# Products with V raised in the scheduler's order, and a third staging buffer for weights

## The chip, the cores and the metric

One core of a Trainium2 chip runs the whole program. The metric is the device time of one execution in microseconds (us), from the first to the last instruction and what lies around them. TensorE (PE) does the matmuls, VectorE (DVE) and ScalarE (ACT) the elementwise work, GpSimd (POOL) next to nothing here; SyncE (SP) issues nearly all DMAs. Each engine takes its own instructions in the order in which they were laid down when the program was built.

## What is computed

Causal attention over 4 batches of 8 heads, 576 positions, head size 64, mixed with a linear memory, and behind it two feed-forward blocks (FFN) on the 2304 resulting rows of width 512:

```python
scores = scale * q @ k.T            # causal mask, softmax
local = a @ v
q_p = phi(q)                        # elu(q) + 1
mem_out = (q_p @ M_prev) / (q_p @ z_prev + 1e-06)
x = g * mem_out + (1 - g) * local   # g = sigmoid(beta) per head
x = softplus(x @ w_in) @ w_out      # 512 -> 2048 -> 512
x = relu(x @ w_in2) ** 2 @ w_out2   # 512 -> 2048 -> 512
```

q, k, v, M_prev, z_prev are 32-bit floats. The weights come as 64-bit words; each is turned into a 32-bit float and split into a high and a low 16-bit half. Other operands of matmuls are split likewise, and a product is three matmuls (high by high, high by low, low by high), summed in PSUM.

## The kernel before

**Attention.** The rows are cut into 18 chunks of 128 (8 for each pair of batches, and a ninth that holds the last 64 rows of both). `CH`, `EXT` and `GRP` list them: a chunk has `EXT` = 128 to 640 key positions in reach, and its 8 heads are done in steps of `GRP` heads (4, 2 or 1, so that a step has about 512 columns). `prep_k`, `prep_q`, `prep_phi`, `prep_v` and `prep_m` cast, split and transpose a chunk's inputs, one part of the next chunk at a time between the steps. The loads go into tiles of one buffer each in the pool `att`, issued from SP; for chunk 1, k, q and v go into extra tiles in the pool `stage`, so that they need not wait for those of chunk 0.

**A step.** `emit_s` (line 281) computes a head's scores on PE into one of two banks of `s_ps` (306), lets DVE add the mask and take the row minimum (311), and ACT take the exponential with its row sum (315); the result is in `Pt`, two buffers. `emit_p` (320) splits it (ACT 327, DVE 328) and transposes it into `PT`, four buffers: for chunks 0 and 1 with PE and an ACT copy (196, 197), for all others with a transposing DMA from SP (190). `emit_pv` (335) stands `LAG` = 4 steps behind in the program. At a chunk's first head it calls `prep_n` (258), the memory norm: 16 matmuls `nps` (264) into a PSUM tile of the pool `mm`, whose three buffers the PE transposes use too, and three DVE steps (270 to 272) into `cc`. Then it does the memory products (343) and the products with V (351) into `pvt`, a tile of one buffer for four heads. After four heads `emit_x` (362) scales `pvt` on DVE into `xt` (371), which frees `pvt`, adds the two parts (378), and after eight heads splits the sum (382, 383) and transposes it to x.

**Feed-forward.** The first FFN runs in blocks of 256 rows (two chunks). A unit `h` is 24 matmuls on W1 (431 to 433) and the softplus on ACT and DVE (435 to 442); a block has eight. A unit `x` is 96 matmuls on W2 (448 to 450); for block 0 the same work stands in four quarters `xq` (485 to 487), 48 matmuls each, so that quarter a needs only the weight pieces 8a to 8a + 7 and those before. The 32 weight pieces of 512 KB are loaded by `load_piece` into `wst` (`NST` = 2 buffers, pool `stage`) and split by `split_piece` (404) with DVE (414, 415, 416, 419) and ACT (418) by way of `wcv`, two buffers. The load of piece i + `NST` is written right behind the split of piece i. The second FFN (702 to 722) starts when the first has ended.

**The order of the work.** A loop at the end of the function writes the steps of attention and the FFN units of earlier blocks in turn, in shares by estimated time. The build then runs a list scheduler with a model of times: at each moment an engine takes, of what the model holds to be ready, the instruction that stands first. `tc.high_priority(n)` lets what is written inside stand as if it were n instructions earlier in the program. Weight splits have 2000 (`HW`), `emit_x` 200 (`HXE`), scores 50 (`HS`), the split and transpose of p 50 (`HP`). Products with V, with all of `emit_pv`, and the FFN units have none. The result is one fixed order for each engine.

Of the kernel before, what the change touches and what calls it, by code (L numbers as in the profile page):

```python
# [21 lines left out]
FR = 0.4  # L22
W1R = 1
B1Q = 3
HS, HP, HXE, HW = 50, 50, 200, 2000

LOE = 99
TQ = 2
# [4 lines left out]
KVB = 9  # L33
SPB = 2
WCB = 2
NST = 2
PTB = 4
PB = 2
P16 = 2
# [4 lines left out]
def kernel(  # L44
# [49 lines left out]

    stage_cm = tc.tile_pool(name="stage", bufs=NST, reuse_waits="tile")
    w1_cm = tc.tile_pool(name="w1", bufs=1, side="right", reuse_waits="tile")
# [16 lines left out]
    stage = stage_cm.__enter__()  # L113
# [45 lines left out]
    def segs(g):  # L159
        x = CH[g]  # L160
        if len(x) == 2:
            return [(x[0], P * x[1], 0, P)]
        return [(2 * x[0] + i, 4 * P, i * R, R) for i in range(2)]

    def lo_eng(g):
        return dve if g < LOE else pool

    def load(nm, g, pool_=None):
        if g >= NC or (nm, g) in raw:
            return  # L170
        src = {"q": q, "k": k, "v": v}[nm]
        t = (pool_ or att).tile([P, H, D], F32, name="raw" + nm, bufs=1)
        for b, s0, r0, n in segs(g):
            sp.dma_start(out=t[r0:r0 + n], in_=src[b, :, s0:s0 + n, :].rearrange("h p d -> p h d"))
        raw[nm, g] = t
    def load_m(g):
        for b, s0, r0, n in (segs(g) if g < NC else []):
            if s0 == 0:
                t = att.tile([P, EMAX], F32, tag="Pt", name="mraw", bufs=PB)[:, :HD].rearrange("p (h d) -> p h d", h=H)
                for i in range(2):  # L180
                    sp.dma_start(out=t[i * D:(i + 1) * D], in_=M_prev[b].rearrange("h d e -> d h e"))
                raw["m", g] = t

    def transp(g, out, in_, lim):
        nblk = in_.shape[1] // P
        if g >= lim:
            step = nblk if nblk <= 12 else nblk // 2
            for a in range(0, nblk, step):
                e = a + step
                sp.dma_start_transpose(out=out[:, a:e], in_=in_[:, a * P:e * P])  # L190
            return
        for a in range(0, nblk, 8):
            e = min(nblk, a + 8)
            ps = mm.tile([P, 8, P], F16, tag="mm", name="tps")
            for i in range(a, e):
                pe.transpose(ps[:, i - a], in_[:, i * P:(i + 1) * P], ident)
            act.activation(out[:, a:e], ps[:, :e - a], AF.Copy)

    def prep_q(g):
        r = raw["q", g]  # L200
        qT[g] = att.tile([P, 2 * H, P], F16, name="qT", bufs=2)
        if g < TP:
            qn = att.tile([P, H, 2, D], F16, tag="qn", name="qn")
            act.activation(qn[:, :, 0, :], r, AF.Copy)
            lo_eng(g).tensor_tensor(qn[:, :, 1, :], r, qn[:, :, 0, :], ALU.subtract)
            transp(g, qT[g][:, :H], qn.rearrange("p h t d -> p (h t d)"), TP)
            ps = mm.tile([P, H, P], F16, tag="mm", name="tps")
            for h in range(H):
                for t in range(2):
                    pe.transpose(ps[t * D:(t + 1) * D, h], qn[:, h, 1 - t], ident)  # L210
            act.activation(qT[g][:, H:], ps, AF.Copy)
            return
        qn = att.tile([P, 2, H, 2, D], F16, name="qn")
        act.activation(qn[:, 0, :, 0, :], r, AF.Copy)
        lo_eng(g).tensor_tensor(qn[:, 0, :, 1, :], r, qn[:, 0, :, 0, :], ALU.subtract)
        dve.tensor_copy(qn[:, 1, :, 1, :], qn[:, 0, :, 0, :])
        dve.tensor_copy(qn[:, 1, :, 0, :], qn[:, 0, :, 1, :])
        transp(g, qT[g], qn.rearrange("p a h t d -> p (a h t d)"), TP)
# [9 lines left out]
    def prep_v(g):  # L228
        r = raw.pop(("v", g))
        V[g] = att.tile([P, 2, H, D], F16, name="V", bufs=KVB)  # L230
        act.activation(V[g][:, 0], r, AF.Copy)
        dve.tensor_tensor(V[g][:, 1], r, V[g][:, 0], ALU.subtract)
# [12 lines left out]
    def prep_phi(g):  # L245
        r = raw.pop(("q", g))
        e = att.tile([P, H, D], F32, tag="prod", name="phie")
        act.activation(e, r, AF.Relu, scale=-1.0)
        act.activation(e, e, AF.Exp, scale=-1.0)
        f = att.tile([P, H, D], F32, name="phi")  # L250
        dve.scalar_tensor_tensor(f, r, 0.0, e, ALU.max, ALU.add)
        fn = att.tile([P, H, 2, D], F16, name="phin")
        act.activation(fn[:, :, 0, :], f, AF.Copy)
        lo_eng(g).tensor_tensor(fn[:, :, 1, :], f, fn[:, :, 0, :], ALU.subtract)
        phiT[g] = att.tile([P, H, P], F16, name="phiT", bufs=2)
        transp(g, phiT[g], fn.rearrange("p h t d -> p (h t d)"), TP)

    def prep_n(g):
        ps = mm.tile([P, H], F32, tag="mm", name="nps")
        for b, s0, r0, n in segs(g):  # L260
            for h in range(H):
                for t in range(2):
                    i = b * H + h
                    pe.matmul(
                        ps[r0:r0 + n, h:h + 1], phiT[g][:, h, r0:r0 + n], zc[:, t, i:i + 1],
                        start=(t == 0), stop=(t == 1),
                    )
        cc = att.tile([P, 2, 2, H // 2], F32, name="cc", bufs=3)
        c2 = cc[:, :, 1, :]
        dve.tensor_scalar(c2, ps.rearrange("p (a h) -> p a h", a=2), 1.0e-6, None, ALU.add)  # L270
        dve.reciprocal(c2, c2)
        dve.tensor_tensor(c2, c2, gM.rearrange("p (a h) -> p a h", a=2), ALU.mult)
        cc_t[g] = cc

    def kblocks(g):
        x = CH[g]
        if len(x) == 2:
            return [[POS[x[0], i]] for i in range(x[1] + 1)]
        return [[POS[2 * x[0] + j, i] for j in range(2)] for i in range(4)] + [[g]]
# [55 lines left out]
    def emit_pv(g, h):  # L335
        if h == 0:
            prep_n(g)
        if h % 4 == 0:
            pvt[g] = pvp.tile([P, 2, H // 2, D], F32, name="pvt")
        for t in range(2):  # L340
            for b, s0, r0, n in segs(g):
                o = pvt[g][r0:r0 + n, 1, h % 4]
                pe.matmul(o, phiT[g][:, h, r0:r0 + n], Mt[b][:, t, h, :], start=(t == 0), stop=(t == 1))
        o = pvt[g][:, 0, h % 4]
        t, o0, nb = PT.pop((g, h))
        for i, ks in enumerate(kblocks(g)):
            n = P // len(ks)
            for y, z in ((0, 0), (0, 1), (nb, 0)):
                for x, kb in enumerate(ks):
                    r = slice(x * n, (x + 1) * n)  # L350
                    pe.matmul(  # L351
                        o[r], t[:, o0 + i + y, r], V[kb][:, z, h, :],
                        start=(i == 0 and y + z == 0), stop=(i == nb - 1 and y > 0),
                    )
# [143 lines left out]
    load("k", 0)  # L498
    load("q", 0)
    load("k", 1, stage)  # L500
    load("q", 1, stage)
    load("v", 0)
    gates()
    z_setup()
# [22 lines left out]
    prep_k(0)  # L527
    prep_q(0)
    prep_phi(0)
    prep_v(0)  # L530
    load_m(0)
    load("v", 1, stage)
    for i in range(NST):
        pieces[i] = load_piece(order[i], (moe_w_in, moe_w_out), sp, stage)
    prep_m(0)
# [8 lines left out]
    def attn_step(s):  # L544
        if s < len(steps):
            g, h = steps[s]
            G = GRP[g]
            with tc.high_priority(HS):
                emit_s(g, h)
            nst = H // G  # L550
            i = h // G
            for part in range(4):
                if part * nst // 4 == i:
                    prep_part(g + 1, part)
            with tc.high_priority(HP):
                emit_p(g, h)
        for g, h0 in pv_at.get(s, ()):
            for h in range(h0, h0 + GRP[g]):
                emit_pv(g, h)
                if h % 4 == 3:  # L560
                    with tc.high_priority(HXE):
                        emit_x(g, h // 4)
# [25 lines left out]
    def run_unit(u):  # L588
# [8 lines left out]
        else:  # L597
            i = u[1]
            with tc.high_priority(HW):
                split_piece(order[i], pieces.pop(i), (W1, W2), stage, on_pool=False)  # L600
            if i + NST < 2 * NPC:
                pieces[i + NST] = load_piece(order[i + NST], (moe_w_in, moe_w_out), sp, stage)

    s = nw = 0
    while s <= ready_step(0):
        attn_step(s)
        s += 1
        while nw < 2 * NPC and nw < W1R * s:
            run_unit(("w", nw))
            nw += 1  # L610
# [82 lines left out]
    while t0 < NT:  # L693
# [3 lines left out]
        for f in range(NFC):  # L697
# [10 lines left out]
            g = [bp.tile([P, 512], F16, name=f"gg{t}_{f}", bufs=1) for t in range(2)]  # L708
# [47 lines left out]
```

## Time and profile before

| | |
|---|---|
| median of 3 runs | 1000.85 us (997.05 to 1002.72) |
| the profiled execution's own time | 1001.6 us |
| its span, first to last instruction | 999.8 us |
| mean granted TensorE clock | 0.953 |
| PE busy | 911.8 us (91%) |
| DVE busy | 583.1 us (58%) |
| ACT busy | 545.2 us (55%) |
| DMA moved | 101.00 MB |

A matmul's busy time overlaps with that of its neighbours, so the time of a line on PE is not to be added to that of another; the busy time of the whole engine is. The clock is a share of full speed: 1.0 is the upper level of 2.4 GHz, 0.5 the lower of 1.2. The page cuts the span into 40 slices of 25 us. In a timeline, a row has the start, the length, the engine and line, the operation, what it writes from what, and in brackets how long the engine was idle before it and what ended that. SPq is SP's queue of DMA issues.

### The profile page before, as it was taken

The numbers are of one execution on the slowest core, as the hardware profiler recorded it, in microseconds if no ns is written. First come the engines' busy times: TensorE is split into PE (matmuls) and PEld (weight loads), VectorE is DVE, ScalarE is ACT, GpSimd is POOL, SyncE is SP. The second block draws the span as 40 slices with busy tenths as digits, with TensorE's granted clock in tenths as the row PEclk, the third lists the DMA queues.
The fourth block names the chain that finished last, engine by engine and source line by source line (L and its number), as shares of the span: only waits on it lengthen the run. The fifth ranks groups of instructions, "written<-read, shape, count | busy, mean of one in ns | idle before, by whom it ended". The sixth has DMA issues, their size and how long they took to land.

```text
span 999.8 us, 20668 instructions
## 1 busy us (share of the span) xinstructions
PE 911.8 (91%) x8436; PEld 642.3 (64%) x8436; DVE 583.1 (58%) x1359; ACT 545.2 (55%) x1090; POOL 2.2 (0%) x10
## 2 busy tenths in 40 slices
PE   3335988899999999999999999999999999999998
PEld 2234877788678888999887887444444444444483
DVE  6888998878546786767756399980240141042040
ACT  8765787779548696867867284640340241142050
POOL 0000000000000000000000000000000000000000
PEclk8555999999899999999999999999999999999999
DMA  9999898787568985655743365520000000000000
GB/s 202 215 221 226 179 165 177 140 125 126 98 99 134 191 156 109 110 83 95 126 86 65 87 205 170 171 82 32 11 1 22 22 1 11 32 1 11 22 13 22
DMA packets 283216, 101.00 MB, mean 101 GB/s; under 512 B 248048, under 2 KB 280816, under 8 KB 283120
## 3 DMA queue, kind: packets, MB, share of 16 engines
q1 hardware_dynamic: 282880, 99.65, 49.3%
q8 instruction: 66, 1.08, 0.5%
q14 instruction: 30, 0.25, 0.1%
q10 hardware_dynamic: 240, 0.02, 0.0%
HBM read 48.78 MB, written 4.72 MB: 54 GB/s over the span
## 4 chain that ended last, share of the span: by engine, by line
PE 65%; DMA 12%; DVE 12%; ACT 7%; issue 3%; SPq 1%; ACTq 0%; DVEq 0%
PE h2ps L703 6%; PE h2ps L704 6%; PE h2ps L702 6%; PE ops L718 6%; PE ops L720 6%; PE ops L719 6%; PE xps L448 4%; PE xps L449 4%; PE xps L450 4%; PE s_ps L306 4%; PE hps L431 3%; PE hps L432 3%; PE hps L433 3%; DMA rawk<-in_k_dram 2%; PE pvt L351 2%
## 5 line engine op out<-in xcount | busy, mean ns | idle before, releaser
L709 DVE CAST gg<-r 128x512 f16<-128x512 f32 (+1 forms) x80 | 32.0, 399 | 232.5 <-ACT r L707 206.7
L431 PE MATMUL hps<-x,W 128*128 128x256 f16 x576 | 157.9, 274 | 2.7 <-DMA x<-xn 1.6
L433 PE MATMUL hps<-x,W 128*128 128x256 f16 x576 | 157.8, 274 | 0.1
L432 PE MATMUL hps<-x,W 128*128 128x256 f16 x576 | 157.9, 274 | 0.0
L448 PE MATMUL xps<-g,W 128*128 128x256 f16 x512 | 139.8, 276 | 3.2 <-ACT g L441 3.1
L449 PE MATMUL xps<-g,W 128*128 128x256 f16 x512 | 140.4, 275 | 1.6 <-DVE g L442 1.6
L450 PE MATMUL xps<-g,W 128*128 128x256 f16 x512 | 140.5, 276 | 0.0
L306 PE MATMUL s_ps<-KT,qT 128*128 128x128 f16 (+2 forms) x992 | 94.6, 227 | 38.9 <-DVE cs L311 34.7
L315 ACT ACTIVATE Pt<-Pt,cs 128x128 f32<-128x128 f32 (+4 forms) x144 | 84.2, 585 | 66.9 <-DVE cs L311 66.6
L704 PE MATMUL h2ps<-x,W 128*128 128x512 f16 (+1 forms) x320 | 114.5, 358 | 0.0
L702 PE MATMUL h2ps<-x,W 128*128 128x512 f16 (+1 forms) x320 | 114.5, 358 | 0.0
L703 PE MATMUL h2ps<-x,W 128*128 128x512 f16 (+1 forms) x320 | 114.5, 358 | 0.0
L719 PE MATMUL ops<-W,gg 128*128 128x512 bf16 x288 | 109.0, 379 | 0.0
L720 PE MATMUL ops<-W,gg 128*128 128x512 f16 x288 | 109.0, 379 | 0.0
L718 PE MATMUL ops<-W,gg 128*128 128x512 f16 x288 | 108.5, 379 | 0.0
L722 ACT ACTIVATE osb<-ops 128x512 f32<-128x512 f32 x18 | 10.7, 597 | 169.3 <-PE ops L720 169.3
L306 PEld LDWEIGHTS <-qT 128*128 128x128 f16 (+1 forms) x992 | 64.5, 106 | 55.4 <-issue 42.0
L328 DVE TENSOR_TENSOR p<-Pt,p 128x512 f16<-128x512 f32 (+2 forms) x104 | 69.1, 665 | 28.0 <-ACT p L327 27.4
L706 ACT ACTIVATE r<-h2ps 128x512 f32<-128x512 f32 (+1 forms) x80 | 44.1, 552 | 75.2 <-PE h2ps L704 75.1
L351 PE MATMUL pvt<-V,PT 128*128 128x64 f16 (+1 forms) x1392 | 65.8, 198 | 12.8 <-DMA PT<-p 10.7
L311 DVE CUSTOM_DVE_ANT_0 Pt<-s_ps,mask 128x128 f32<-128x128 f32 (+3 forms) x128 | 61.9, 483 | 12.3 <-PE s_ps L306 11.6
L327 ACT ACTIVATE p<-Pt 128x512 f16<-128x512 f32 (+2 forms) x104 | 63.1, 607 | 9.4 <-DMA PT<-p 8.0
(117 smaller groups left out, 1642.7 us busy)
## 6 DMA issues: line engine op xcount, KB each, us to landing
wst<-in_moe_w_in_dram SPq DMA_DIRECT2D x32, 512.0 KB, 4.7
wst<-in_moe_w_out_dram SPq DMA_DIRECT2D x32, 512.0 KB, 4.2
rawk<-in_k_dram SPq DMA_DIRECT2D x16, 256.0 KB, 4.1
rawq<-in_q_dram SPq DMA_DIRECT2D x16, 256.0 KB, 4.1
rawv<-in_v_dram SPq DMA_DIRECT2D x16, 256.0 KB, 4.3
out_dram<-osb SPq DMA_DIRECT2D x16, 256.0 KB, 2.0
PT<-p SPq DMA_TRANSPOSE x100, 3.4
mraw<-in_M_prev_dram SPq DMA_DIRECT2D x8, 128.0 KB, 4.3
```

The lines of the kernel that those rows point to most:

```text
L306: pe.matmul(o[x * n:(x + 1) * n], qT[g][:, t * H + h, x * n:(x + 1) * n], KT[kb][:, h, a - j * P:e - j * P], start=(t == 0), stop=(t == 1),)
L431: pe.matmul(o, wh, x[:, c], start=(c == 0), stop=False)
L432: pe.matmul(o, wh, x[:, NCC + c], start=False, stop=False)
L433: pe.matmul(o, wl, x[:, c], start=False, stop=(c == NCC - 1))
L448: pe.matmul(ps, wh, gh, start=(f == f0), stop=False)
L449: pe.matmul(ps, wh, gl, start=False, stop=False)
L450: pe.matmul(ps, wl, gh, start=False, stop=(f == f1 - 1))
L702: pe.matmul(ps[:, :n], wh, xh, start=(c == 0), stop=False)
L703: pe.matmul(ps[:, :n], wh, xl, start=False, stop=False)
L704: pe.matmul(ps[:, :n], wl, xh, start=False, stop=(c == NCC - 1))
L719: pe.matmul(ps, gh, W4[1][:, f, :], start=False, stop=False)
L720: pe.matmul(ps, gl, W4[0][:, f, :], start=False, stop=(f == NFC - 1))
```

## The change

Scores stand 100 instructions earlier instead of 50. All that `emit_pv` writes gets a block of its own at 300. `NST` goes from 2 to 3. q and v of chunk 1 are loaded into the usual tiles of `att` instead of extra tiles in `stage`, and their loads are written behind the last reader of chunk 0's: q behind `prep_phi(0)`, v behind `prep_v(0)` as before. k of chunk 1 keeps its extra tile. In space, the two tiles of 2 KB a partition that go from `stage` make room for the third `wst` of 4 KB.

```diff
-HS, HP, HXE, HW = 50, 50, 200, 2000
+HS = 100
+HP = 50
+HXE = 200
+HW = 2000
+HV = 300
...
-NST = 2
+NST = 3
...
     load("k", 1, stage)
-    load("q", 1, stage)
     load("v", 0)
...
     prep_phi(0)
+    load("q", 1)
     prep_v(0)
     load_m(0)
-    load("v", 1, stage)
+    load("v", 1)
...
             for h in range(h0, h0 + GRP[g]):
-                emit_pv(g, h)
+                with tc.high_priority(HV):
+                    emit_pv(g, h)
                 if h % 4 == 3:
                     with tc.high_priority(HXE):
                         emit_x(g, h // 4)
```

## Rows read from the trace of the kernel before

**Rows 1.** The page, 40 slices of the span: granted TensorE clock in tenths.

```profile
PEclk8555999999899999999999999999999999999999
```

**Rows 2.** Windows: length; busy us of PE, PEld, DVE, ACT, POOL; clock; DMA; GB/s.

```profile
0.00:93.80 93.80, 35.21 (x378) 26.86 (x379) 76.48 (x209) 62.86 (x139) 2.23 (x10) 0.58 1.05 213
93.80:262.00 168.20, 154.79 (x1982) 135.74 (x1982) 147.12 (x352) 132.86 (x268) 0.00 (x0) 0.97 0.80 152
262.00:400.00 138.00, 130.61 (x1539) 109.19 (x1538) 87.12 (x236) 89.61 (x203) 0.00 (x0) 1.00 0.80 135
400.00:566.00 166.00, 164.26 (x2246) 145.19 (x2245) 109.75 (x256) 118.50 (x236) 0.00 (x0) 1.00 0.51 89
566.00:999.80 433.80, 426.91 (x2298) 225.35 (x2296) 162.61 (x310) 141.37 (x246) 0.00 (x0) 0.99 0.16 51
```

**Rows 3.** Timeline of PE, 26 to 112 us.

```profile
33.09 0.34 PE L351 MATMUL pvt<-V,PT 128*128 128x64 f16 x3 [1.83 <-ACT PT L197]
...
51.35 0.61 PE L264 MATMUL nps<-zc,phiT 128*128 128x1 f16 x16
...
63.12 0.29 PE L343 MATMUL pvt<-Mt,phiT 128*128 128x64 f16 x2 [1.23 <-DVE xt L371]
...
78.68 0.29 PE L343 MATMUL pvt<-Mt,phiT 128*128 128x64 f16 x2 [2.38 <-DVE xt L371]
...
93.82 0.37 PE L431 MATMUL hps<-x,W 128*128 128x256 f16 x1 [1.11 <-ACT x L197]
...
97.18 0.42 PE L432 MATMUL hps<-x,W 128*128 128x256 f16 x1
...
97.56 0.27 PE L431 MATMUL hps<-x,W 128*128 128x256 f16 x1
...
100.73 0.27 PE L433 MATMUL hps<-x,W 128*128 128x256 f16 x1
```

**Rows 4.** Timeline of DVE, 30 to 130 us.

```profile
55.98 0.16 DVE L272 TENSOR_TENSOR cc<-cc,gM 128x8 f32<-128x8 f32 x1
...
57.41 0.68 DVE L371 TENSOR_TENSOR xt<-pvt,cc 128x512 f32<-128x512 f32 x1
```

**Rows 5.** DMA issues, 400 to 566 us: tile, operation, count, median us to landing.

```profile
PT<-p SPq DMA_TRANSPOSE x39, 3.2
```

**Rows 6.** Timeline of ACT, 53 to 94 us.

```profile
53.79 1.00 ACT L197 ACTIVATE PT<-tps 128x1024 f16<-128x1024 f16 x1
...
92.74 1.02 ACT L197 ACTIVATE x<-tps 128x1024 f16<-128x1024 f16 x1 [0.67 <-PE tps L196]
```

**Rows 7.** Timeline of DVE: last pass of the eighth and of the sixteenth weight piece.

```profile
54.52 0.66 DVE L419 TENSOR_TENSOR W<-wcv,W 128x512 bf16<-128x512 f32 x1
...
96.32 0.68 DVE L419 TENSOR_TENSOR W<-wcv,W 128x512 bf16<-128x512 f32 x1
```

**Rows 8.** PE's waits, 117 to 400 us: total us, times, longest.

```profile
PE pvt L351 <- DMA PT<-p: 10.7, 14, 1.3
```

**Rows 9.** DMA issues, 117 to 400 us.

```profile
PT<-p SPq DMA_TRANSPOSE x54, 3.6
```

**Rows 10.** PE's waits, 0 to 93.8 us.

```profile
PE s_ps L306 <- DVE cs L311: 30.3, 21, 5.7
```

**Rows 11.** DVE's waits, 0 to 93.8 us.

```profile
DVE wcv L414 <- DMA wst<-in_moe_w_out_dram: 4.9, 4, 2.0
```

**Rows 12.** Timeline of all engines, 0 to 70 us.

```profile
3.79 0.97 SPq L174 DMA_DIRECT2D rawq<-in_q_dram  x1
...
8.24 0.69 DVE L251 SCALAR_TENSOR_TENSOR phi<-rawq,phie 128x512 f32<-128x512 f32 x1 [0.49 <-ACT phie L249]
...
25.79 0.37 PE L306 MATMUL s_ps<-KT,qT 128*128 128x128 f16 x2 [1.58 <-ACT V L231]
```

**Rows 13.** DMA issues, 0 to 93.8 us: KB each, median us to landing.

```profile
rawq<-in_q_dram SPq DMA_DIRECT2D x5, 256.0 KB, 5.1
```

## The prediction, made before the change was run

> **What bounds the kernel now.** I read the slices of the page first, then the windows, then the timeline of each engine around the places where the windows change character.
>
> The clock row is the quickest sight of the shape [rows 1]: TensorE was granted half speed in slices 2 to 4, full speed from then on. The windows tell why [rows 2]. Until 93.8 us PE is busy 35.21 us of 93.8, so 58.6 us are idle; from 93.8 to 262 it idles 13.4 us, from 262 to 400 7.4 us, from 400 to 566 1.7 us, and behind that 6.9 us. From 93.8 us on the end is set by the sum of PE's work, and only idle PE time can be taken out. Two thirds of that lies ahead of 93.8 us, where the first matmul of the first FFN block starts [rows 3]. So the question is what that matmul waits for, and how much work is ready when it starts sooner.
>
> It waits for the x of chunks 0 and 1, and that comes late for one reason which the timeline shows. The products with V of chunk 0's first half run at 33.09 us. The 16 tiny matmuls of the memory norm (nps, line 264), written just ahead of them, run at 51.35 us [rows 3]; the DVE line that needs them (272) follows at 55.98, and xt, which empties the only pvt tile, at 57.41 us [rows 4]. All other products of chunks 0 and 1 stand behind that: chunk 1's first at 63.12, its last half at 78.68 [rows 3].
>
> **Products with V at 300.** The block now holds all that `emit_pv` issues: nps and its three DVE steps, the memory products and the products with V. From 400 to 566 us there are 2246 matmuls, 256 DVE and 236 ACT instructions [rows 2] for 39 transposes of p, one a step [rows 5]: 70 a step. 300 is 4.3 steps, and the products stand 4 steps behind their scores: they will run as soon as their transposed p is there.
>
> At the start this is the gain. With nps no longer at 51, xt of chunk 0 moves to the thirties, pvt is free, and chunk 1's last half waits for its own p alone. ACT copies that p's transpose at 53.79 [rows 6], done at 54.8. Today it is 15.1 us from the start of that half's products (78.68) to the end of the last copy of x (92.74 + 1.02) [rows 3, 6]; I keep these 15.1, since DVE is as full as before, and get 70 us. The first FFN matmul starts about 24 us sooner.
>
> What can run then? One quarter of block 0: 2 units of 24 matmuls on W1 and 48 on W2, on the first eight weight pieces, the last of which is ready at 54.52 + 0.68 us [rows 7]. The second quarter wants the sixteenth piece, at 96.32 today. At full clock 29 matmuls go from 97.56 to 100.73 us, 0.109 us each [rows 3]; 96 of them are **10.5 us** of PE work moved into idle time. That is the main term. Its bounds: 0 if the order does not move, 10.5 on today's pieces.
>
> The clock adds a little. From 93.82 to 97.18 us 16 matmuls went at 0.21 each [rows 3], so 1.7 us are lost in the warm-up, which would now fall into idle time: **1.7 us**, between 0 and 4.5 (half of the 8.9 us that PE works in 24 us at the share of the first window).
>
> At the back the same edit costs. Between 117 and 400 us products already stand at the landing: 14 waits for the transposed p, 10.7 us, among 54 transposes [rows 8, 9]. From 400 to 566 us PE's waits hold none of this kind, and now the 39 transposes there come to stand so too. Bounds: 0, and 0.76 us (the mean wait) for each of 39, 29.8 us. Taken: as often as in the earlier stretch (14 of 54), but landing takes 3.2 us there against 3.6 [rows 5, 9]; so 0.36 us for 10 of them, **3.6 us**.
>
> **Scores at 100 in place of 50.** This moves scores, mask step and exp up by 0.7 of a step, past p's split and the preparations on DVE and ACT. PE waits 30.3 us for DVE's mask step in the first stretch [rows 10], with nothing else to do. Two Pt buffers hold the scores to two steps ahead. If the scores win more DVE turns, p and prepared chunks are later. I take 0: it helps the start that is counted above and does not raise the work that is ready. Bounds 2 us either way (three turns of 0.68, the copy's length in [rows 7]).
>
> **Three staging buffers.** Eight pieces take 41.8 us, from 54.52 to 96.32, 5.2 us each [rows 7]. A third in flight could bring the sixteenth and later pieces forward, and with them the other quarters. Bounds: 0, and the 13.4 us that PE idles from 93.8 to 262. Nearest row: in the first window DVE waited 4.9 us in all for pieces of w_out [rows 11]; I take **4 us**. The price is on DVE: splits stand ahead of all else, DVE is busy 76.48 of 93.8 us, and each early piece pushes attention back by its four passes (up to 2.7 us at 0.68). Even three of them leave x at 78 us, and the 10.5 us still fit before 93.8.
>
> **q and v of chunk 1 in the usual buffers.** q's load is issued at 3.79 us today [rows 12]. Now it waits until phi of chunk 0 has read rawq (8.24 + 0.69), and lands 5.1 us later [rows 13], at 14.0. The scores of chunk 1 start at 25.79 [rows 12]: 12 us of cover. If that were gone, the cost is 5 us. v follows its chunk's split likewise, and is wanted at 63.12 now, in the forties then. The later loads of q and v shift by the same few us, under the same cover. On SP these loads and a third weight load come into one queue ahead of transposes; I cost this at nothing here because PE is idle there. The space balances.
>
> **Sum.** 10.5 + 1.7 + 4 - 3.6 = 12.6 us less than the profiled execution's 1001.6 us: 989.0. That execution was 0.75 over the median 1000.85, so **988**.
>
> **Rivals.**
> *The gain is given back, or never made.* The weights set the pace: the DMA engines' share is 1.05 up to 93.8 us and 0.80 up to 262 [rows 2], so a third load only shares them. Then later quarters start when they do now, the 10.5 us that ran early are missing behind, PE idles that much more, and the time is 1000. For it speaks the share; against it, the 4.9 us of DVE's wait [rows 11], little beside 93.8. The Trainium skill (Perfetto Trace Analysis, What "DMA-bound" means) says that where the DMA engines bind, larger descriptors are what matters; by it the third buffer alone brings nothing and the sum would be 992. Here the shares agree that they are full, but the short DVE wait does not. Also here: nps takes its PSUM tile from the pool of the PE transposes, three buffers; if it still gets none before 51 us, the start stays at 93.8 and only 4 and 3.6 remain, 1000. Together 0.18.
>
> *Slower: PE stands at the products.* The engine runs in order, so a product placed at its landing holds up the FFN matmuls behind it. Place: the steps from 400 us on. Price: up to 29.8 us; with 12.2 us still won at the start, 1018. It turns the sign by more than 0.5% from 17.2 us on, 0.44 us for each of the 39. For it: the slack there, which this edit removes, is why no wait is seen. Against: where the products stand at the landing already, three of four do not wait. The Trainium skill (DMA: Bandwidth & Descriptors, Queues, rings and completion order) has each DMA engine take a ring's descriptors in order, so that a transpose waits behind a load issued before it on SP. The trace agrees in direction, 3.6 us with loads about and 3.2 with few. Chance 0.19.
>
> *More than forecast.* The third buffer brings the whole 13.4 us and the clock 4.5: 972. This is part of the faster share.
>
> **How the numbers follow.** Faster by over 0.5% (about what a measurement of this kernel can tell, 5 us: below 995.8) has my forecast and the larger gain, 0.63; within it the first rival, 0.18; slower the second, 0.19. The range goes from the larger gain, less 2 us for the spread of runs, 970, to the upper edge of no change, 1006, plus the same 2: 1008. Alone, the forecast's own range is 972 to 996.
>
> **What would show it.** Right: nps before 40 us, xt before 42, the first FFN matmul between 62 and 80, PE busy over 45 us up to 93.8, the sixteenth piece before 92, the last scores' landing waits from 400 us on below 8 us in all. Wrong: the first FFN matmul still after 88; or that start, but PE idle from 93.8 to 262 over 24 us (first rival); or waits for the transposed p over 28 us in the whole trace (second). If PE's idle time in the first 93.8 us falls and the end does not, I have mistaken where the work was short.

## The result, and the profile after

The changed kernel takes 992.37 us (median of 12 runs, 989.44 to 1001.07), the kernel before 1001.89 in the same comparison: a ratio of 0.9908 (0.9882 to 0.9934), some 9 us faster. The profiled execution of after has an own time of 997.09 us and a span of 995.3, so it lies 4.7 us above its median, and the two profiles side by side show only 4.5 us of the gain.

First the windows of after, with the columns of [rows 2]; the edges are the same but for the end.

```profile
0.00:93.80 93.80, 39.91 (x401) 30.27 (x402) 81.14 (x226) 64.95 (x144) 2.23 (x10) 0.98 1.13 228
93.80:262.00 168.20, 154.78 (x1982) 135.58 (x1981) 143.58 (x334) 129.61 (x263) 0.00 (x0) 0.95 0.80 148
262.00:400.00 138.00, 130.48 (x1661) 115.13 (x1660) 94.35 (x256) 97.02 (x217) 0.00 (x0) 1.00 0.79 135
400.00:566.00 166.00, 161.35 (x2149) 140.23 (x2147) 106.39 (x243) 111.58 (x225) 0.00 (x0) 0.98 0.57 96
566.00:995.30 429.30, 421.12 (x2234) 220.94 (x2250) 159.45 (x303) 140.00 (x245) 0.00 (x0) 0.99 0.15 47
```

PE idles 53.9, 13.4, 7.5, 4.7 and 8.2 us in the five windows, against 58.6, 13.4, 7.4, 1.7 and 6.9 before. The first window gave 4.7 us, not the 12 forecast, and the fourth took 3 back. The clock of the first window, 0.98 against 0.58, is no gain: the first clock record of after stands at 85.8 us, and the page takes the clock as full where it has none. The first FFN matmuls of after still follow one another at 0.21 us (three from 90.79 to 91.43) and last 0.42, as those from 93.82 to 97.18 in [rows 3] did before the full clock came; that is the lower level, 1.2 GHz. (In the last window 18 matmul records are missing, 8418 for 8436; at 0.22 us each they are 4 us of the 8.2.)

The timeline of PE in after, 26 to 92 us; line numbers are 5 higher than before:

```profile
26.24 0.34 PE L356 MATMUL pvt<-V,PT 128*128 128x64 f16 x3 [0.86 <-ACT PT L202]
...
49.36 0.29 PE L201 MATMUL tps<-ident,p 128*128 128x128 f16 x1 [0.62 <-ACT p L332]
49.44 0.61 PE L269 MATMUL nps<-zc,phiT 128*128 128x1 f16 x16
...
57.67 0.27 PE L348 MATMUL pvt<-Mt,phiT 128*128 128x64 f16 x2 [0.62 <-DVE xt L376]
...
77.04 0.29 PE L348 MATMUL pvt<-Mt,phiT 128*128 128x64 f16 x2 [0.62 <-DVE xt L376]
...
90.79 0.42 PE L436 MATMUL hps<-x,W 128*128 128x256 f16 x1
...
91.43 0.42 PE L436 MATMUL hps<-x,W 128*128 128x256 f16 x1
```

Beside [rows 3]: the products of chunk 0's first half moved from 33.09 to 26.24 us. That is not the work of their priority. The same row in two kernels of the experiments below, products_alone (before with the priority) and after_no_products (after without it):

```profile
32.73 0.34 PE L352 MATMUL pvt<-V,PT 128*128 128x64 f16 x3 [0.93 <-ACT PT L198]
```

```profile
26.23 0.34 PE L356 MATMUL pvt<-V,PT 128*128 128x64 f16 x3 [0.86 <-ACT PT L202]
```

The memory norm nps moved from 51.35 to 49.44 only. So chunk 1's products still stand behind it (57.67 for 63.12, the last half 77.04 for 78.68), and the first FFN matmul came from 93.82 to 90.79, 3.0 us earlier, not 24.

The timeline of DVE in after (last pass of the eighth weight piece, xt of chunk 0, last pass of the sixteenth piece), and then one row of before:

```profile
47.07 0.69 DVE L424 TENSOR_TENSOR W<-wcv,W 128x512 bf16<-128x512 f32 x1
...
56.93 0.69 DVE L376 TENSOR_TENSOR xt<-pvt,cc 128x512 f32<-128x512 f32 x1
...
95.20 0.68 DVE L424 TENSOR_TENSOR W<-wcv,W 128x512 bf16<-128x512 f32 x1
```

```profile
105.08 0.69 DVE L419 TENSOR_TENSOR W<-wcv,W 128x512 bf16<-128x512 f32 x1
```

xt stands at 56.93 for 57.41 [rows 4]. The last row corrects the prediction: its sixteenth piece at 96.32 [rows 7] was the fifteenth; counted through, the sixteenth ends at 105.8 before and 95.9 after, 9.9 us sooner. (So the 41.8 us between the two rows of [rows 7] are seven pieces of 6.0 us, and not eight of 5.2.)

The waits in after that answer to [rows 8] (PE, 117 to 400 us), to "none of this kind" (PE, 400 to 566), to [rows 10] and to [rows 11] (PE up to 91, DVE up to 93.8), and the transposes of [rows 9] and [rows 5]:

```profile
PE pvt L356 <- DMA PT<-p: 11.1, 14, 1.8
```

```profile
PE pvt L356 <- DMA PT<-p: 4.5, 8, 0.8
```

```profile
PE s_ps L311 <- DVE cs L316: 32.3, 21, 4.3
```

```profile
DVE wcv L419 <- DMA wst<-in_moe_w_in_dram: 0.2, 1, 0.2
```

```profile
PT<-p SPq DMA_TRANSPOSE x55, 3.3
```

```profile
PT<-p SPq DMA_TRANSPOSE x36, 3.2
```

Products now stand at the landing behind 400 us too: 8 of 36 wait there, 4.5 us. DVE's wait for pieces of w_out, 4.9 us, is gone, and one of 0.2 us remains. PE's wait for the mask step on DVE is as long as before.

### The profile page after: what moved, and what is told of

Same layout as the page of the kernel before. It is cut to its first block, busy times and chain, and to the rows that moved or that the text cites. A ratio compares the mean times of both kernels' runs of the same rounds, so it can differ in the third digit from the quotient of the medians.

```text
span 995.3 us, 20666 instructions
## 1 busy us (share of the span) xinstructions
PE 907.6 (91%) x8418; PEld 642.2 (65%) x8436; DVE 584.9 (59%) x1359; ACT 543.2 (55%) x1090; POOL 2.2 (0%) x10
## 4 chain that ended last, share of the span: by engine, by line
PE 67%; DMA 14%; DVE 9%; ACT 5%; issue 3%; SPq 1%; ACTq 0%; DVEq 0%
PE ops L726 7%; DMA PT<-p 6%; PE h2ps L710 6%; PE h2ps L709 6%; PE h2ps L708 6%; PE ops L724 6%; PE ops L725 6%; PE xps L454 4%; PE xps L455 4%; PE xps L453 4%; PE s_ps L311 3%; PE hps L438 3%; PE hps L437 3%; PE hps L436 3%; PE pvt L356 3%
## 5 line engine op out<-in xcount | busy, mean ns | idle before, releaser
L436 PE MATMUL hps<-x,W 128*128 128x256 f16 x576 | 160.1, 278 | 3.5 <-DVE cc L275 2.1
L438 PE MATMUL hps<-x,W 128*128 128x256 f16 x576 | 160.0, 278 | 0.0
L437 PE MATMUL hps<-x,W 128*128 128x256 f16 x576 | 160.0, 278 | 0.0
L311 PE MATMUL s_ps<-KT,qT 128*128 128x128 f16 (+2 forms) x992 | 83.8, 225 | 35.9 <-DVE cs L316 35.3
L725 PE MATMUL ops<-W,gg 128*128 128x512 bf16 x270 | 102.3, 379 | 0.0
L311 PEld LDWEIGHTS <-qT 128*128 128x128 f16 (+1 forms) x992 | 59.2, 105 | 47.7 <-issue 43.1
L356 PE MATMUL pvt<-V,PT 128*128 128x64 f16 (+1 forms) x1392 | 62.1, 199 | 16.7 <-DMA PT<-p 15.6
```

The lines of the kernel that those rows point to most:

```text
L311: pe.matmul(o[x * n:(x + 1) * n], qT[g][:, t * H + h, x * n:(x + 1) * n], KT[kb][:, h, a - j * P:e - j * P], start=(t == 0), stop=(t == 1),)
L436: pe.matmul(o, wh, x[:, c], start=(c == 0), stop=False)
L437: pe.matmul(o, wh, x[:, NCC + c], start=False, stop=False)
L438: pe.matmul(o, wl, x[:, c], start=False, stop=(c == NCC - 1))
```

## The experiments

**How the tables are read.** The stretch behind the last W2 matmul of the first FFN is 377.6 to 377.8 us in every kernel here whose numbers are given, so the difference lies ahead of it. From the first FFN matmul to that one, I took the time from each matmul's start to the next and subtracted the pace of its kind at full clock (0.1095 us for the FFN's 256 columns, 0.0535 for scores of 128, 0.0285 for products with V or with the memory, 0.026 for nps). What is left over is put under one cause: PE at 1.2 GHz (by the clock records); a gap of over 0.15 us; or a step between a matmul with 64 columns of weights and one with 128 (below). The number of cases is in parentheses; "nps" and "first FFN" are starts in us, "last W2" is the end of that stretch, the three columns between are lost us. Each row is one profiled execution, and such a one lies up to 5 us off its median (after 4.7 above, loads_alone 4.2 below), so differences of a few us in it are no results. Two things stand in no column. In nine of the kernels (all but before, after, buffer_alone and the two with every norm early) the clock records begin only after the first FFN matmul; there the first 15 to 26 matmuls at 0.21 us, 1.5 to 2.6 us, are missing from "half clock". And matmuls with 64 columns that stand together run faster than the pace taken here (see the steps between widths).

| kernel | nps | first FFN | half clock | gaps | 64/128 steps | last W2 |
|---|---|---|---|---|---|---|
| before | 51.4 | 93.8 | 6.0 | 29.7 (33) | 20.2 (193) | 622.1 |
| after | 49.4 | 90.8 | 13.4 | 34.0 (36) | 10.1 (103) | 617.7 |
| products_alone | 47.0 | 92.7 | 4.9 | 32.7 | 11.2 (113) | 614.0 |
| scores_alone | 51.3 | 93.0 | 6.7 | 29.7 | 14.5 (142) | 616.9 |
| buffer_alone | 49.3 | 93.6 | 7.8 | 22.8 | 16.6 (159) | 611.0 |
| loads_alone | 42.9 | 90.9 | 4.9 | 20.1 (21) | 15.2 (149) | 602.4 |
| after_no_products | 49.4 | 93.4 | 9.0 | 26.7 | 14.7 (142) | 616.2 |
| after_two_buffers | 42.8 | 91.4 | 10.5 | 35.4 | 12.1 (119) | 622.3 |
| after_norm01 | 15.1 | 74.7 | 11.4 | 46.2 (44) | 11.1 (111) | 618.1 |
| after_norm_early | 15.1 | 77.6 | 42.6 | 48.4 | 13.8 (138) | 654.4 |
| before_norm_early | 17.1 | 72.0 | 59.4 | 74.7 | 17.2 (166) | 695.6 |
| scores_ext | 50.3 | 91.7 | 4.8 | 29.3 (30) | 7.6 (78) | 603.7 |
| loads_scores_ext | 42.9 | 90.9 | 3.1 | 22.7 (22) | 7.9 (82) | 594.7 |
| scores_51 | 51.3 | 93.1 | 8.6 | 27.8 | 19.6 (186) | 624.0 |

All these kernels compute everything that the reference does. Each ratio is to the kernel before in the same comparison, with its 95% interval.

**One part at a time.** *products_alone*, on before:

```diff
+HV = 300
-                emit_pv(g, h)
+                with tc.high_priority(HV):
+                    emit_pv(g, h)
```

> The kernel before with the block at 300 round emit_pv alone. The whole change gave a ratio of 0.9908, 9.5 us, though nps stayed at 49 us and the first FFN matmul moved only from 93.8 to 90.8. Theory A (the gain is the products': attention ends about 10 us sooner and PE has no long stretch without ready work): ratio 0.990 to 0.994, last product with V near 555 us in place of 565. Theory B (the gain is the third buffer's): ratio 0.998 to 1.004, and the products at their landing cost something at the back. Theory C (scores at 100 make it): same as B here.

Measured: 994.12 us, 0.9938 (0.9914 to 0.9962). Waits for the transposed p from 91 to 620 us: 20.4 us in 22, against 10.7 in 14 before. So the products do come to their landing and lose 10 us there, and the kernel is faster all the same: the ratio is in the range of theory A, and the last product with V starts at 557.5 us for 565.1 before. The start explains 1.1 us of it; the largest change in the table is the steps between widths, 9.0 us less.

*scores_alone*, on before: `HS` 50 becomes 100.

> The kernel before with scores at 100 alone. Theory C: ratio 0.990 to 0.994. Theories A and B: 0.998 to 1.003, with PE's waits for the mask step in the first 93.8 us (30.3 us) as long as before within 3 us.

Measured: 995.97 us, 0.9950 (0.9930 to 0.9969). Costed at nothing, it is worth 5 us alone, between the ranges of the theories; PE's wait for the mask step is 29.5 us, as before. The start moved 0.8 us, gaps not at all, the steps between widths from 20.2 to 14.5.

*buffer_alone* has `NST` 3 and the moved loads of q and v of chunk 1, as shown; *loads_alone* has the moved loads and two buffers, so it lacks the first two lines:

```diff
-NST = 2
+NST = 3
...
-    load("q", 1, stage)
...
     prep_phi(0)
+    load("q", 1)
...
-    load("v", 1, stage)
+    load("v", 1)
```

> The kernel before with three staging buffers and the loads of q and v of chunk 1 moved, no priorities changed. Theory B: ratio 0.990 to 0.994, the 32nd weight piece 8 us or more before 194 us. Theories A and C: 0.996 to 1.002.

> The kernel before with the loads of q and v of chunk 1 moved and two staging buffers. All theories: 0.998 to 1.003, the cover of 12 us over q holds; if the later q is on the path, the first score of chunk 1 comes up to 5 us after 25.8 us and the ratio is 1.003 to 1.006.

Measured: buffer_alone 990.02 us, 0.9898 (0.9871 to 0.9926), at the edge of theory B; loads_alone 986.09, 0.9850 (0.9820 to 0.9880). The part that I costed at nothing is the largest of the change, outside every range that I had given for it, and on top of it the third buffer costs 4 us. Where it starts is seen on SP's queue, first in before (behind the row at 3.79 us of [rows 12]), then in loads_alone:

```profile
4.80 1.18 SPq L174 DMA_DIRECT2D rawv<-in_v_dram  x1
6.02 1.83 SPq L181 DMA_DIRECT2D mraw<-in_M_prev_dram  x2
7.89 0.62 SPq L174 DMA_DIRECT2D rawv<-in_v_dram  x1
8.56 1.81 SPq L395 DMA_DIRECT2D wst<-in_moe_w_in_dram  x2
```

```profile
3.86 0.97 SPq L174 DMA_DIRECT2D rawv<-in_v_dram  x1
4.87 1.85 SPq L181 DMA_DIRECT2D mraw<-in_M_prev_dram  x2
6.76 1.17 SPq L395 DMA_DIRECT2D wst<-in_moe_w_in_dram  x2
```

The rows at 3.79 and 7.89 are chunk 1's q and v for the extra tiles; both are gone from there. V of chunk 0 is issued 0.9 us sooner, the first pieces 1.8. Then the attention's chain of steps carries it on. These are the last mask steps of chunk 0 on DVE, of before, of loads_alone and of buffer_alone:

```profile
25.45 0.28 DVE L311 CUSTOM_DVE_ANT_0 Pt<-s_ps,mask 128x128 f32<-128x128 f32 x1
```

```profile
23.59 0.28 DVE L311 CUSTOM_DVE_ANT_0 Pt<-s_ps,mask 128x128 f32<-128x128 f32 x1
```

```profile
28.46 0.29 DVE L311 CUSTOM_DVE_ANT_0 Pt<-s_ps,mask 128x128 f32<-128x128 f32 x1
```

With the loads alone they end 1.9 us sooner and nps starts 8.5 us sooner; with a third buffer, three pieces come to DVE ahead of the mask steps, which end 4.9 us later than with two, and nps falls back to 49.3. In all kernels but products_alone and the three with an earlier norm, the start of nps goes with the loads and the buffers (42.8 or 42.9, 49.3 or 49.4, and 50.3 to 51.4 where nothing of either is done), and not with the priority of the products. Behind the start, loads_alone loses 9.6 us less in gaps and 5.0 less in steps between widths. Why a start 3 us earlier leaves so many fewer gaps was not tried further, so beyond the start the cause of the 14.5 us is open.

**One part taken out of the change.** *after_no_products* is after without the block at 300, *after_two_buffers* is after with `NST` 2.

> The changed kernel without the block round emit_pv. Theory: the products' priority wins steps between 64 and 128 columns and loses as much in waits for the transposed p (15.6 us in 22 waits behind 91 us against 3.6 in 5 with the buffer alone): ratio to the kernel before 0.988 to 0.993, the same as the changed kernel within 0.3%, waits under 9 us, steps over 130. Rival (the products' priority is worth its 6 us here too): 0.994 to 0.998.

> The changed kernel with two staging buffers. Loads moved alone gave 0.985, loads moved with the third buffer 0.990. Theory: the third buffer costs about 4 us, and without it the change gives 0.983 to 0.988. Rival (the third buffer gives what the prediction credits it with): 0.992 to 0.997.

Measured: after_no_products 997.24 us, 0.9973 (0.9951 to 0.9994); after_two_buffers 998.22, 0.9984 (0.9964 to 1.0005). Within the change, the priority of the products is worth 6.5 us (0.9973 to 0.9908) and the third buffer 7.6 (0.9984 to 0.9908), though the same buffer cost 4 in buffer_alone. Both kernels missed what I expected: after_no_products came out in its rival's range, after_two_buffers above both of its ranges. after_no_products differs from buffer_alone in `HS` alone: there scores at 100 cost 7.5 us (0.9898 to 0.9973), while alone they gave 5. Only the products' priority has the same price in both places, 6.5 us alone and 6.5 within. For the buffer and the scores each edit deals a new order, and the price depends on the rest of it.

**Is it the order of nps that holds the start?** *after_norm01* writes the memory norm of chunks 0 and 1 right behind their `prep_phi` and leaves all else of the change as it is:

```diff
-        if h == 0:
+        if h == 0 and g > 1:
             prep_n(g)
...
             prep_phi(g)
+            if g == 1:
+                prep_n(g)
...
     prep_phi(0)
+    prep_n(0)
```

> The changed kernel with the memory norm of chunks 0 and 1 alone written behind prep_phi; all other chunks as in the changed kernel. Written early for all chunks, nps of chunk 0 ran at 15 us and the first FFN matmul at 78, but the end came 38 us later, with FFN units and transposes held up all along. Theory P (the tail came from nps holding PSUM tiles of mm ahead of the FFN units in the written order, chunk after chunk; the early start itself pays as the prediction had it): first FFN matmul between 62 and 80, ratio to the kernel before 0.976 to 0.986. Rival G (an early start is given back: until the next pieces and chunks are there PE has one quarter to do, then idles and falls to half clock): first FFN matmul between 62 and 80, but PE idles over 12 us between that and 150 us (3.1 in the changed kernel from 91 on), ratio 0.988 or more.

Measured: 997.87 us, 0.9961 (0.9943 to 0.9979), 5 us worse than after. Its timeline of PE:

```profile
12.61 1.06 PE L201 MATMUL tps<-ident,phin 128*128 128x128 f16 x8
15.09 0.59 PE L269 MATMUL nps<-zc,phiT 128*128 128x1 f16 x16
...
74.66 0.37 PE L436 MATMUL hps<-x,W 128*128 128x256 f16 x1 [1.20 <-ACT x L202]
```

Both halves of the main term stand apart here. The start does hang on nps: at 15.09 it runs, xt of chunk 0 is at 37.3 and the first FFN matmul at 74.66, as the prediction had wanted (70). But the gain is given back, as rival G had it. Windows of after_norm01, then of after, over the same times (columns of [rows 2]):

```profile
91.00:120.00 29.00, 23.57 (x249) 20.14 (x247) 27.77 (x69) 21.56 (x46) 0.00 (x0) 0.88 1.02 226
120.00:150.00 30.00, 20.93 (x235) 17.07 (x235) 29.17 (x71) 19.09 (x43) 0.00 (x0) 0.83 0.95 207
```

```profile
91.00:120.00 29.00, 26.89 (x313) 22.71 (x312) 26.13 (x65) 22.36 (x46) 0.00 (x0) 0.85 1.11 221
120.00:150.00 30.00, 28.97 (x352) 26.02 (x351) 25.57 (x62) 20.73 (x44) 0.00 (x0) 1.00 0.91 173
```

DVE is busy 29.17 of 30 us from 120 to 150, and PE idles 9.1 us there (1.0 in after) and 5.4 from 91 to 120 (2.1). PE's two longest groups of waits from 74.7 to 150:

```profile
PE pvt L356 <- DMA PT<-p: 10.0, 5, 3.9
PE xacc L490 <- ACT g L446: 3.9, 1, 3.9
```

The FFN work that started early ran out of prepared work behind it. By the windows it is DVE, which splits the weights, masks the scores and has its part in the softplus, that sets the pace up to 150 us; the DMA engines' share is much the same in both kernels (1.02 for 1.11, 0.95 for 0.91). The longest of the waits, first on DVE, then on SP's queue, then on PE:

```profile
116.59 0.69 DVE L333 TENSOR_TENSOR p<-Pt,p 128x512 f16<-128x512 f32 x1
```

```profile
117.31 1.23 SPq L195 DMA_TRANSPOSE PT<-p  x1
```

```profile
122.68 0.35 PE L356 MATMUL pvt<-V,PT 128*128 128x64 f16 x6 [3.91 <-DMA PT<-p]
```

The transpose goes out as soon as DVE has finished p, so SP's queue does not hold it; the seven that are issued from 110 to 138 us go out 0.02 to 0.44 us behind that pass. Nor does the landing take longer on the whole: from 105 to 150 us its median is 4.2 us for 4.3 in after. DVE itself waits 0.8 us in that time. All this points to DVE; no run gave it less to do. In this kernel the earlier start only moved PE's idle time behind it.

*after_norm_early* and *before_norm_early* write the norm of every chunk behind its `prep_phi`, in after and in before.

> The changed kernel with the memory norm (prep_n) written behind prep_phi, so that nps takes its PSUM tile of the pool mm ahead of the transposes of p. In the changed kernel nps runs at 49.4 us right beside the transposes of p of step 3, and chunk 1's at 65.3 beside those of xn: as if PSUM tiles of that pool were handed out in the order in which they are written, whatever the priority. If that is why the start did not move: nps before 25 us, xt of chunk 0 before 40, first FFN matmul between 62 and 80, and, by the prediction's main term, 8 to 12 us off the changed kernel (ratio to the kernel before 0.979 to 0.983). Rival (DVE or the weights set the start or the pace): nps early, but the first FFN matmul after 85, or a start near 70 with less than 3 us off the end.

> The kernel before with prep_n written behind prep_phi and nothing else. If the place in the pool was the whole obstacle: first FFN matmul between 62 and 82 us and 6 to 12 us off (0.988 to 0.994). Rival: products at no priority still stand behind the scores of chunk 2, first FFN matmul at 85 or later, ratio 0.997 to 1.003.

Measured: 1030.41 us, 1.0299 (1.0270 to 1.0328), and 1074.37, 1.0732 (1.0704 to 1.0759). The first FFN matmul comes at 77.6 and 72.0 us, 16 and 22 us sooner than before, and the kernels are 28 and 72 us slower. The slices of the page show where (after_norm_early):

```profile
PEclk9658877999999789999999899999999999999999
```

TensorE falls back to 1.2 GHz again and again; 42.6 us are lost so, and 48.4 in gaps. An early start alone does not do this: after_norm01 starts earlier than after_norm_early, has much the same gaps (46.2 us) and loses 11.4 us at 1.2 GHz. The starts came as I had expected, the ends did not. Which resource the early norms of the later chunks hold was not tried.

**What the steps between widths cost.** Chunks 8 and 17 hold the last 64 rows of two batches each, and a matmul on their q or p takes the rows of one batch: 64 columns of weights (the form 128*64 in a row), where all others have 128. In before, the scheduler lays chunk 8's scores between W2 matmuls one by one. Timeline of PE in before, then in after at the same time:

```profile
264.17 0.24 PE L306 MATMUL s_ps<-KT,qT 128*64 128x128 f16 x1
264.34 0.28 PE L448 MATMUL xps<-g,W 128*128 128x256 f16 x1
264.56 0.24 PE L306 MATMUL s_ps<-KT,qT 128*64 128x128 f16 x1
264.73 0.28 PE L449 MATMUL xps<-g,W 128*128 128x256 f16 x1
264.94 0.24 PE L306 MATMUL s_ps<-KT,qT 128*64 128x128 f16 x1
```

```profile
264.34 0.53 PE L311 MATMUL s_ps<-KT,qT 128*64 128x128 f16 x7
264.71 0.27 PE L455 MATMUL xps<-g,W 128*128 128x256 f16 x1
264.82 0.27 PE L453 MATMUL xps<-g,W 128*128 128x256 f16 x1
```

A pair takes 0.39 us (264.17 to 264.56 to 264.94); by the paces of the two kinds it would be 0.1095 + 0.0535 = 0.163. So a step costs some 0.11 us, and PE counts as busy meanwhile: no view of waits shows it. It is the change of width that costs: in before some 500 steps between kinds of equal width lose under 3 us in all, 193 between widths 20.2. The Trainium skill (TensorEngine Tiling (Array Packing), Key Properties) says that changing the tiling mode drains TensorE, and gives no time for it. The trace fits this, with 0.11 us a step; that a matmul with 64 columns is such a change of mode, and the lost time the drain, no run here shows.

A mixed score loses something else that the table does not count. Where 64-column scores stand together, two start 3 or 4 ns apart and the next two 56 ns later (starts in the traces of before and scores_ext), so two take the time of one. In before 114 of the 320 such scores run without a partner, in scores_ext, below, 34.

*scores_ext* takes only these scores out of the mixture, on before:

```diff
-            with tc.high_priority(HS):
+            with tc.high_priority(1000 if EXT[g] > 512 else HS):
```

> The kernel before, and only the scores of chunks 8 and 17 (the two that hold the last 64 rows of both batches, and so work on half the array) at 1000 in place of 50. In the kernel before PE goes 193 times from a matmul of 64 columns to one of 128 or back between the first FFN matmul and the last of W2, and each such step costs about 0.105 us over the matmul's own time, 20.2 us in all; in the changed kernel it is 103 times, 10.1 us. Theory W (this is most of what the products' priority wins): the steps fall under 140, at least 5 us off, ratio 0.990 to 0.996. Rival (the steps only take the place of other idle time): the steps fall, ratio 0.998 to 1.003.

Measured: 985.32 us, 0.9853 (0.9824 to 0.9882). 78 steps instead of 193, 12.6 us less lost in them, of 16.3 us by which the stretch from the first FFN matmul to the last W2 matmul is shorter; gaps 29.3 for 29.7. The gain is larger than the range that I gave to theory W. The score matmuls alone in windows from 250 to 300 us (length; busy of PE, of DVE; clock; DMA; GB/s), before and scores_ext:

```profile
250.00:300.00 50.00, 15.10 (x140) 6.32 (x9) 0.93 0.61 99
```

```profile
250.00:300.00 50.00, 7.37 (x146) 7.71 (x14) 1.00 0.83 150
```

PE's busy time on 146 matmuls is half of that on 140, with 120 of 64 columns in both. (The clock of 0.93 in before is a small part of that.)

*loads_scores_ext* puts this beside the moved loads, with two buffers and none of the change's priorities.

> Loads of q and v of chunk 1 moved, two buffers, and the scores of chunks 8 and 17 at 1000. If both gains are the mechanisms that I take them for (an earlier start of the attention's chain; fewer steps between widths) and independent, they add: 0.978 to 0.983, better than the changed kernel. Rival (each is one lucky order of the scheduler): 0.985 to 0.995.

Measured: 975.14 us (972.98 to 976.89), 0.9748 (0.9722 to 0.9775), the best here. It is more than I expected of gains that add (0.978 to 0.983), and less than the two in full: 0.9850 times 0.9853 is 0.9705. The two edits attack mainly different columns of the table (gaps 22.7, steps 7.9), but the moved loads alone had shortened the steps too, by 5.0 us.

**How much is chance?** *scores_51* has `HS` 51, which puts a matmul of another line at 1056 of PE's 8436 places, for no purpose.

> The kernel before with scores at 51 in place of 50: one instruction's place, no purpose. It shows what a change of order without a reason is worth. If the orders that the scheduler makes differ in time by chance: a ratio outside 0.997 to 1.003. If the gains measured here come from their mechanisms: inside.

Measured: 1000.53 us, 0.9980 (0.9961 to 0.9998). This is one draw, and it changes the order at fewer places than the change does, so the size of chance is only sampled. The runs above say more: scores at 100 gave 5 us in one order and cost 7.5 in another, the third buffer gave 7.6 and cost 4, some 12 us apart each. The 14.5, 15.4 and 25.6 us of loads_alone, scores_ext and loads_scores_ext lie above that. The 9 us of the change are clear of the noise of measurement, but no larger than what one edit's price differed by between two orders.

## Why the prediction was right, and where it was wrong

The forecast was 988 us in a range of 970 to 1008, faster with 0.63. It is 992.37, faster by 9 us. Sign and size came out near, but by the marks that the prediction set itself its reason was wrong: of its six marks for right only the landing waits were met (4.5 us from 400 us on, below 8). PE is busy 39.91 us up to 93.8, not over 45, and the sixteenth piece is ready at 95.9, not before 92. That the number is near is luck: of the 12.2 us at the start PE's idle time gave 4.7, and effects that the sum did not hold took the place of the rest.

**The step that failed** is the first: "With nps no longer at 51, xt of chunk 0 moves to the thirties ... The first FFN matmul starts about 24 us sooner." nps runs at 49.44, xt at 56.93, the first FFN matmul at 90.79: 3.0 us sooner, and in the "still after 88" that it called wrong. The case where nps "still gets none before 51 us" was in the first rival. In all eleven kernels with the norm in its old place nps starts 0.08 to 0.11 us behind the first matmul of the transpose of p for chunk 1's last half (49.36 and 49.44 in after), which takes a tile of the same pool and is written ahead of it, whatever the products' priority; written earlier (after_norm01), it runs at 15.09. That the pool hands its tiles out in the order in which they were asked for is the reading that fits; the builder's own record was not seen. I had put the whole of `emit_pv` 4.3 steps forward, because the block holds it, and had named the shared tile in a rival without following who asks for it first. Even on the products of chunk 0's first half the priority did nothing at the start: 32.73 us in products_alone for 33.09 in before.

**And the term behind it would have failed too.** With the start at 74.66 us in after_norm01, 16.1 us before that of after, the stretch behind it is 16.5 us longer, the last W2 matmul ends at 618.1 for 617.7, and the medians are 5 us apart the wrong way. The early matmuls came back as idle time, 11.4 us more of it from 91 to 150, as the first rival had it. The rival blamed the weights' transfers; the windows and the longest wait point to DVE, busy 29.17 of 30 us. I had counted what work is ready when PE starts sooner, and not who prepares the work after that.

**The clock, 1.7 us:** not found. At half clock after loses 13.4 us between the first FFN matmul and the last W2 matmul, before 6.0.

**Products at their landing, -3.6 us from 400 us on:** 4.5 measured, in 8 waits of 36 for 10 of 39. This step held, and the slower rival at 18 us of further waits did not come.

**Third buffer, +4 us:** 7.6 within the change, -4 beside the moved loads alone. The price on DVE that I named, up to 2.7 us per piece, was seen: chunk 0's mask steps end 4.9 us later. That DVE would wait less is right. Its waits for pieces up to 93.8 us in after_two_buffers, against 0.2 us in after:

```profile
DVE wcv L419 <- DMA wst<-in_moe_w_out_dram: 6.0, 3, 4.2
DVE wcv L419 <- DMA wst<-in_moe_w_in_dram: 2.4, 3, 1.9
```

The Trainium skill (Perfetto Trace Analysis, What "DMA-bound" means) says that large descriptors are what matter where the DMA engines bind. The prediction's first rival took from it that this buffer alone would bring nothing. Within the change the runs disagree with that rival: 7.6 us, and 228 GB/s up to 93.8 us for 220 with two buffers. No run changed the size of the descriptors.

**Scores at 100, 0 within 2:** 5 us gained alone, 7.5 lost inside; the bounds were too narrow. **Moved loads, 0:** 14.5 us gained alone; the start is 2.9 us earlier, and why the gaps and the steps behind it fall as well is open. I asked only whether chunk 1's q and v would still be in time, and not what stands behind them in SP's queue at the start, where each load delays all the later ones.

**What I left out altogether:** the steps between 64 and 128 columns, 20.2 us in before and 10.1 in after. In the pair of profiles that is the one cause that shrank by much (10.1 us), beside the start (3.0); half clock (7.4 more) and gaps (4.3 more) took most of it back. That these steps cost time is shown by scores_ext. That they are what the change's 9 us are made of is not shown: the four sum to 1.4 us of the 4.4 between the two profiles, after's profile lies 4.7 us above its median, and no run took the steps alone out of the change. So what the 9 us consist of stays open.

## What to carry to other kernels

Before a gain is put on a raised priority, follow every tile that the moved block must get from a pool shared with other work, and look at which engine prepares the work that PE would reach sooner: here an earlier start on a full DVE was handed back. Where a scheduler deals a new order at each edit, one part's price in one order is no price in another. Cost an edit that takes something away from the front of a queue by all that stands behind it. And where a scheduler mixes matmuls of different weight widths one by one, keep them in blocks: one line that did that, with the moved loads, gave 25 us where the whole change gave 9.

## What the runs showed of the hardware

A step between matmuls of 64 and of 128 columns of weights costs about 0.1 us (20.2 us over 193 steps in before, 7.6 over 78 in scores_ext), hidden in busy time; one between two kinds of equal width under 0.006 us (under 3 us over some 500 in before). Two 64-column scores that stand together take the time of one (starts 3 or 4 ns apart, the next two 56 ns later, in before and scores_ext). With the norm of every chunk early, TensorE lost 42.6 us at 1.2 GHz in after_norm_early and 59.4 in before_norm_early, against 6.0 in before; the sum of the gaps does not tell this loss, since after_norm01 had 46.2 us of gaps for 48.4 in after_norm_early and lost 11.4.
